# Down projection of a gated FFN: nine of eleven pairs of f tiles in a seven-product block form, with a transposed output turned back through DRAM

## The chip, the cores and the metric

The kernel runs on one core of a Trainium2 chip. The metric is the device time of one execution in microseconds (us). Three runs of the kernel before gave 745.83, 746.61 and 747.37 us; the median is 746.61.

## The reference

A layer on x of 2048 tokens and 512 channels: pre-norm attention with a compressive memory, then a pre-norm gated feed-forward, all in fp32. Cut to what matters:

```python
h  = x + attention(layernorm(x))          # 32 heads of 16, 4 segments of 512 tokens
g  = layernorm(h) @ w_gate                # 512 -> 1376
u  = layernorm(h) @ w_up                  # 512 -> 1376
h2 = h + (gelu(g) * u) @ w_down           # 1376 -> 512: the down projection
```

The change touches the last line.

## The kernel before, in words

**Precision.** Each fp32 matrix product is made of three matmuls in fp32r. An operand v is kept as a high part (a ScalarE copy to fp32r) and a low part (v minus the high part, a subtraction on GpSimd or VectorE); `SPLIT` lists high x high, high x low, low x high. So every operand of TensorE that is not a plain load costs a copy and a subtraction. The buffers for such pairs are the `slot`, `stk` and `stq` tiles, plain fp32 tiles of 128x512 are `row` and `vaug`, PSUM banks are `bank`.

**Stages.** The first part, some 390 us, is the attention. The second is the feed-forward (`ffn_weights`, `ffn`, `down`), in two halves p = 0, 1 of 1024 tokens; a half is two blocks s of 512 tokens. The 1376 inner channels are eleven f tiles: ten of 128, one (f = 10) of 96. The second layer norm of the second half (`layer_norm` and `ln2`, with a transposition through `t_dram`, L810 to L819) runs beside the first half of the feed-forward.

**Gate and up.** `ffn` computes gate and up of one f tile for both blocks s in a block form with seven products instead of eight (a Strassen-like scheme): weights a11, a12, a22, s1 to s4, made of gate and up by `ffn_weights` (splits at L1499 and L1501, sums of 256 columns at L1508), times activation blocks made by `ln2`. A product is two matmul groups of three: 7 x 2 x 3 = 42 matmuls per half and f tile, all at L1531. `geglu` (L1547 on) makes h = gelu(g) * u with ScalarE and VectorE, and splits it (ScalarE L1560, GpSimd L1563, for f = 9 VectorE).

**Down.** After a pair of f tiles (f = 10 alone, first pair (0,1), then 10, (2,3), up to (8,9)) `down` takes h as the stationary operand and w_down, split by `split_weight` (L666 to L675), as the moving one: for each of the eight blocks of 128 tokens of the half, three matmuls per f tile (L1596) into one PSUM bank, and one VectorE add into the block's row of sums (L1604), which began as h (L1626). With the last pair (8,9) the row is stored to `out` right after its add (L1609).

**What sets the order.** The program is recorded as operations with their dependencies and then issued in a fixed list, `ORDER`. Each engine works through its instructions strictly as that list gives them; buffers are handed out from pools in the same order. The DMAs are issued by SyncE (SP), but for one of the last stores, which ScalarE issues.

Of the kernel before, what the change touches and what calls it, by code (L numbers as in the profile page):

```python
# [7 lines left out]
F32 = mybir.dt.float32  # L8
# [3 lines left out]
OP = mybir.AluOpType  # L12
# [14 lines left out]
SPLIT = ((0, 0), (0, 1), (1, 0))  # L27

# [463 lines left out]
def infini_geglu(ctx: ExitStack, tc: tile.TileContext, x, wq, wk, wv, wo, beta,  # L492
# [1028 lines left out]
    def ffn(p, f, b):  # L1521
# [14 lines left out]
        def copy(src):  # L1536
            c = Val(PC)
            act(D, prio, lambda: nc.scalar.activation(c.t[:w], src.t[:w], AF.Copy), [src], [c])  # L1538
            return c
# [159 lines left out]
```

## Time and profile before

| what | before |
|---|---|
| median of three runs | 746.61 us |
| span of the profiled execution, first to last instruction | 745.2 us |
| runs above that span | 0.6 to 2.2 us, the median 1.4 |
| TensorE busy | 729.3 us, 98% |
| VectorE busy | 568.5 us, 76% |
| ScalarE busy | 511.5 us, 69% |
| GpSimd busy | 474.5 us, 64% |
| matmuls of gate and up (L1531) begin | 376.0 us |

The profiled execution is one run of its own, of which the span is known; the runs carry a little more around it. PE is TensorE, PEld its weight loads, DVE VectorE, ACT ScalarE, POOL GpSimd. An arrow `<-` stands between what is written and what is read; tile names come without their numbers in the profile.

### The profile page before, as it was taken

To read this page: it belongs to the slowest core of one execution; us is meant where nothing else is said; L and a number is where in the kernel's file an instruction comes from. 1 tells how busy PE (TensorE), PEld (TensorE's weight loads), DVE (VectorE), ACT (ScalarE), POOL (GpSimd) and SP (SyncE) were. 2 spreads that over 40 slices of the span, in tenths; PEclk is the share of its full clock that TensorE was granted. 3 is DMA by queue.
4 is the path that set the end of the run, shared out by engine and by line. 5 is a ranking of instruction groups with operands and counts; after the bars stand their busy time and mean duration, and the time that the engine had idled before them with its cause. 6 is when DMAs were issued, how large, how long until landed. Compare 5 with 4: busy or idle time off the path is not lost.

```text
span 745.2 us, 18708 instructions
## 1 busy us (share of the span) xinstructions
PE 729.3 (98%) x6496; PEld 582.5 (78%) x6496; DVE 568.5 (76%) x1812; ACT 511.5 (69%) x1078; POOL 474.5 (64%) x750
## 2 busy tenths in 40 slices
PE   7999999999999999999999999999999999999998
PEld 6887867777877777876768788888887878888886
DVE  6897879988887898899987547775688756565466
ACT  6898888797767878878676557755586453553641
POOL 5455425564536546876884887868797578659930
PEclk9999999999999999999999999999999999999999
DMA  7756647656657757776756685554334260000003
GB/s 268 203 142 163 173 127 190 177 131 189 175 155 206 211 155 200 185 219 197 194 186 219 215 258 158 108 134 103 106 106 129 67 210 19 0 1 1 0 1 113
DMA packets 89658, 107.92 MB, mean 145 GB/s; under 512 B 31468, under 2 KB 41884, under 8 KB 89564
## 3 DMA queue, kind: packets, MB, share of 16 engines
q1 hardware_dynamic: 89260, 106.34, 50.2%
q8 instruction: 51, 0.84, 0.5%
q10 hardware_dynamic: 304, 0.39, 0.2%
q14 instruction: 43, 0.35, 0.2%
HBM read 57.03 MB, written 23.53 MB: 108 GB/s over the span
## 4 chain that ended last, share of the span: by engine, by line
PE 86%; DVE 8%; ACT 2%; issue 2%; DMA 1%; SPq 0%; DVEq 0%; ACTq 0%
PE bank L1531 28%; PE bank L1596 15%; PE bank L932 9%; PE bank L1272 8%; PE bank L1244 6%; PE bank L1186 5%; PE bank L981 5%; PE bank L1352 3%; PE bank L1345 3%; DVE bank L1196 2%; DVE aside L1196 2%; PE bank L1154 1%; DMA row<-wq 1%; DVE nm L1196 1%; PE bank L798 1%
## 5 line engine op out<-in xcount | busy, mean ns | idle before, releaser
L1250 ACT ACTIVATE row<-bank 128x512 f32<-128x512 f32 x309 | 165.5, 604 | 29.8 <-PE bank L1244 25.4
L1258 POOL TENSOR_SCALAR_AFFINE_SELECT row<-row 128x256 f32<-128x256 f32 (+1 forms) x309 | 105.9, 367 | 89.9 <-ACT row L1250 87.6
L1196 DVE CUSTOM_DVE_ANT_0 aside<-bank,amask 128x384 f32<-128x384 f32 (+2 forms) x384 | 141.7, 419 | 17.4 <-PE bank L1186 10.2
L932 PE MATMUL bank<-slot,slot 64*128 64x512 f32 x720 | 114.3, 403 | 0.0
L1531 PE MATMUL bank<-slot,slot 128*128 128x512 f32 (+1 forms) x399 | 106.1, 391 | 0.0
L1196 DVE CUSTOM_DVE_ANT_0 bank<-bank,amask 128x512 f32<-128x512 f32 x128 | 86.5, 710 | 12.0 <-PE bank L1186 10.1
L1531 PEld LDWEIGHTS bank<-slot,slot 128*128 128x128 f32 (+1 forms) x399 | 73.6, 186 | 17.5 <-issue 0.4
L1501 POOL TENSOR_TENSOR slot<-row,slot 128x512 fp32r<-128x512 f32 (+2 forms) x55 | 61.6, 1125 | 39.9 <-ACT slot L1499 37.6
L1186 PE MATMUL bank<-stk,stq 64*128 64x512 f32 (+3 forms) x512 | 82.0, 331 | 2.6 <-DMA stq<-slot 0.9
L1244 PE MATMUL bank<-stq,stk 64*128 64x384 f32 (+3 forms) x512 | 81.4, 333 | 1.7 <-DVE nm L1196 0.8
L1604 DVE TENSOR_TENSOR row<-row,bank 128x512 f32<-128x512 f32 (+1 forms) x91 | 60.4, 677 | 29.6 <-PE bank L1596 29.2
L1272 PE MATMUL bank<-row,vaug 128*32 128x512 f32 (+3 forms) x988 | 78.8, 436 | 1.2 <-DVE z L1145 0.4
L932 PEld LDWEIGHTS bank<-slot,slot 64*128 64x128 f32 x720 | 73.0, 185 | 6.2 <-DVE nm L1196 0.7
L1186 PEld LDWEIGHTS bank<-stk,stq 64*128 64x128 f32 x512 | 56.5, 185 | 14.4 <-DVE nm L1196 3.7
L1244 PEld LDWEIGHTS bank<-stq,stk 64*128 64x128 f32 x512 | 56.1, 185 | 14.6 <-DVE nm L1196 3.7
L1596 PE MATMUL bank<-slot,slot 128*128 128x512 f32 (+1 forms) x228 | 59.8, 389 | 0.0
L1272 PEld LDWEIGHTS bank<-row,vaug 128*32 128x32 f32 x988 | 30.5, 109 | 34.3 <-issue 27.3
L1531 PE MATMUL bank<-stk,slot 128*128 128x512 f32 (+1 forms) x198 | 54.7, 389 | 0.0
L981 PE MATMUL bank<-slot,slot 64*128 64x256 f32 x672 | 53.4, 284 | 0.0
L672 POOL TENSOR_TENSOR slot<-row,slot 128x512 fp32r<-128x512 f32 (+1 forms) x33 | 42.6, 1293 | 16.0 <-ACT slot L667 15.8
L1538 ACT ACTIVATE row<-bank 128x512 f32<-128x512 f32 (+1 forms) x54 | 31.6, 594 | 28.3 <-PE bank L1531 27.3
L1196 DVE DVE_READ_ACCUMULATOR2_ANT nm<- 128x1 f32 x512 | 50.1, 98 | 0.0
(269 smaller groups left out, 1622.4 us busy)
## 6 DMA issues: line engine op xcount, KB each, us to landing
stq<-slot SPq DMA_DIRECT2D x96, 128.0 KB
stk<-slot SPq DMA_DIRECT2D x94, 128.0 KB
row<-x SPq DMA_DIRECT2D x31, 256.0 KB
pv_dram<-row SPq DMA_DIRECT2D x31, 256.0 KB
row<-r_dram SPq DMA_DIRECT2D x27, 256.0 KB
row<-h_dram SPq DMA_DIRECT2D x23, 256.0 KB
row<-wd SPq DMA_DIRECT2D x17, 256.0 KB
row<-wu SPq DMA_DIRECT2D x16, 256.0 KB
```

The lines of the kernel that those rows point to most:

```text
L932: return nc.tensor.matmul(pm[i].t, w[i].t[rows_of(r), wi, dc * P:(dc + 1) * P], XT[s][dc].t[rows_of(r), xi, :], start=(dc, wi, xi, ph) == ...
L981: return nc.tensor.matmul(pms[n].t[:, 256 * t:256 * t + 256], XT[s][dc].t[rows_of(r), xi, t0:t0 + P], whl[wi].t[rows_of(r), dc // 2, 256 * ...
L1186: nc.tensor.matmul(sa.t[:, c0:c0 + w], sq.t[own, p, i * P:(i + 1) * P], sk.t[own, p, 0:w], start=True, stop=True, tile_position=(64 * a, 0 ...
L1196: nc.vector.tensor_tensor_reduce(out=(sa.t[:, c0:c0 + w] if i > 2 else aside[:, turns[0]:turns[0] + w]), in0=sa.t[:, c0:c0 + w], in1=amask ...
L1244: nc.tensor.matmul(sc.t[:, c0:c0 + D - q0], sk.t[own, p, q0:q0 + P], sq.t[own, p, q0:D], start=True, stop=True, tile_position=(64 * a, 0), ...
L1250: act(w, prio, lambda sc=sc, e=e: nc.scalar.activation(e.t[:, :w], sc.t[:, :w], AF.Exp), [sc, vtab], [e])
L1258: nc.gpsimd.affine_select(v, v, pattern=pat + [[1, P]], compare_op=OP.is_ge, fill=0.0, base=0, channel_multiplier=-1)
L1272: nc.tensor.matmul(pv.t[32 * n:32 * n + 32, kb * P:D], va.t[:, 136 * kb + 17 * j:136 * kb + 17 * j + 32], e.t[:, lo:lo + D - kb * P], star ...
L1501: pool(0.14 + 2.13e-3 * (hi - lo), prio, lambda: nc.gpsimd.tensor_tensor(v.t[:, 1, :hi - lo], r.t[:, lo:hi], v.t[:, 0, :hi - lo].bitcast(F ...
L1531: nc.tensor.matmul(dst.t[:w], v.t[:, wi, c0 + j * w:c0 + (j + 1) * w], b[bk][j].t[:, xi, :], start=first and j == 0 and n == 0, stop=j == ...
L1596: nc.tensor.matmul(pm.t[:, cs], HH[p, f, s].t[:w, hi, t * P:(t + 1) * P], v.t[:w, wi, cs], start=f == fl[0] and n == 0, stop=f == fl[-1] a ...
L1604: dve(W_, prio, lambda a=a, pm=pm, cs=cs, to=to: nc.vector.tensor_tensor(to.t[:, cs], a.t[:, cs], pm.t[:, cs], op=OP.add), [pm, a], [to])
```

## The change

Nine pairs of f tiles take a new way: all five of the first half, and (0,1) to (6,7) of the second. The two single tiles f = 10 and the last pair (8,9) of the second half stay with `down`.

- **Seven products for down** (`down7`). The pair's two f tiles and the two token blocks s form a 2x2 block matrix b11, b12, b21, b22 of h; w_down of the pair is a 2x2 block matrix with 256 output channels to a block. w_down is now stationary and h the moving operand, so the output comes transposed: channels on partitions, tokens along the row. Seven products of 2 x 3 matmuls. VectorE makes four block differences (`sub`), each from two SBUF tiles; seven operands are split (ScalarE copy; low part on GpSimd, in the first three pairs of the first half two of the seven on VectorE). `geglu` no longer splits h for these tiles.
- **Gathering** (`gather`). Each product is added on VectorE from its PSUM bank into one of eight transposed sums; the first product of each sum is a ScalarE copy.
- **Weight blocks** (`wd_prep`, `wd_load`). In the first half GpSimd makes s1 to s4 of a pair (four operations of 256 columns), and all seven blocks are split (ScalarE and GpSimd, 256 columns each); of the first four pairs they go to `wd_dram`, from where the second half loads them. The input `wdp` is w_down with permuted columns, reordered on the host. Eight of the 35 `row` tiles become `half` tiles for the blocks (`halves`).
- **Turning back** (`turned`, `blocks_out`). Once the last pair of a half is gathered, VectorE turns 32x32 blocks (4 x 4 instructions of 128 columns per 512 tokens), 16 DMAs write them to `y_dram` so that the rest of the transposition falls into the addresses, and four loads bring them back by token. f = 10 has put its rows (h plus its share) into `g_dram`; these are loaded and added on GpSimd. In the first half the result is stored to `out`; in the second it is the row of sums to which the pair (8,9) is added before the store.
- The transposition of the second layer norm uses `blocks_out` too (16 short VectorE instructions where four long ones stood). The recorded cost of one VectorE step of the attention rises from 560 to 910, and `ORDER` is a new list for the whole program.

Three places in the order follow, each before and after; numbers behind names are buffers.

VectorE, first half, while the second layer norm of the other half runs. Before: the down adds (L1604) read a `row` tile and a bank, like the steps of `ffn` around them.

```order
L1543 TENSOR_TENSOR row_116<-row_116,bank_69 128x512
L1543 TENSOR_TENSOR bank_71<-row_129,bank_71 128x512
L1604 TENSOR_TENSOR row_135<-row_135,bank_72 128x512
L1604 TENSOR_TENSOR row_106<-row_106,bank_66 128x512
L1543 TENSOR_TENSOR bank_67<-vaug_145,bank_67 128x512
L1551 SCALAR_TENSOR_TENSOR row_129<-row_129,bank_71 128x512
L1604 TENSOR_TENSOR row_120<-row_120,bank_70 128x512
L1556 SCALAR_TENSOR_TENSOR bank_71<-row_129,bank_71 128x512
L1558 SCALAR_TENSOR_TENSOR row_129<-bank_71,row_116 128x512
L1604 TENSOR_TENSOR vaug_142<-vaug_142,bank_72 128x512
```

After, third pair: gathering adds are L1748, block differences L1711, low parts on VectorE L1718, short transposes L716.

```order
L1718 TENSOR_TENSOR slot_81<-row_109,slot_81 128x512
L812 SCALAR_TENSOR_TENSOR ln_167<-bank_70,ln_166 128x4
L1586 SCALAR_TENSOR_TENSOR row_104<-row_104,bank_72 128x512
L1588 SCALAR_TENSOR_TENSOR row_124<-row_124,bank_71 128x512
L1573 TENSOR_TENSOR bank_65<-vaug_140,bank_65 128x512
L1711 TENSOR_TENSOR row_109<-row_124,row_109 128x512
L716 STREAM_TRANSPOSE row_121<-row_134 128x4x32
L1581 SCALAR_TENSOR_TENSOR row_127<-row_127,bank_65 128x512
L1748 TENSOR_TENSOR row_111<-row_111,bank_70 128x512
L1748 TENSOR_TENSOR row_123<-row_123,bank_68 128x512
L748 TENSOR_SCALAR mv_160<-bn_158 128x1
```

The adds are gathering adds now, and between them stand operations that read two SBUF tiles (`row,row` and `row,slot`).

GpSimd, later in the first half. Before: weight splits (L1501), weight sums of 256 columns (L1508), splits of h (L1563).

```order
L1501 TENSOR_TENSOR slot_88<-row_115,slot_88 128x512
L1563 TENSOR_TENSOR stq_98<-vaug_143,stq_98 128x512
L1501 TENSOR_TENSOR slot_74<-row_104,slot_74 128x512
L1508 TENSOR_TENSOR vaug_141<-row_107,vaug_141 128x256
L1508 TENSOR_TENSOR vaug_141<-vaug_141 128x256
L1501 TENSOR_TENSOR slot_86<-row_130,slot_86 128x256
L1501 TENSOR_TENSOR slot_85<-row_107,slot_85 128x512
L1508 TENSOR_TENSOR row_130<-row_130 128x256
L1563 TENSOR_TENSOR stq_97<-row_114,stq_97 128x512
L1508 TENSOR_TENSOR row_130<-row_132,row_130 128x256
L1501 TENSOR_TENSOR slot_84<-row_132,slot_84 128x512
```

After: splits of the blocks of h (L1718), gate and up as before (L1526), and w_down's block sums (L1679) and block splits (L1687).

```order
L1718 TENSOR_TENSOR slot_80<-row_111,slot_80 128x512
L1679 TENSOR_TENSOR row_127<-row_127,row_134 128x256
L1718 TENSOR_TENSOR stq_96<-row_109,stq_96 128x512
L1526 TENSOR_TENSOR slot_85<-row_120,slot_85 128x512
L1526 TENSOR_TENSOR stq_99<-row_115,stq_99 128x512
L1718 TENSOR_TENSOR slot_73<-row_124,slot_73 128x512
L1687 TENSOR_TENSOR half_6807<-row_121,half_6807 128x256
L1718 TENSOR_TENSOR slot_84<-row_105,slot_84 128x512
L1526 TENSOR_TENSOR slot_80<-row_108,slot_80 128x512
L1687 TENSOR_TENSOR half_6812<-row_101,half_6812 128x256
L1718 TENSOR_TENSOR stq_96<-row_125,stq_96 128x512
```

The operations that prepare w_down have come in between, and there are more splits of h.

SyncE at the end of the program. Before: one weight load and the stores of the rows.

```order
L1494 DMA row_102<-wg 128x512
L1609 DMA out_dram<-row_113 128x512
L1609 DMA out_dram<-row_111 128x512
L1609 DMA out_dram<-row_109 128x512
L1609 DMA out_dram<-row_120 128x512
L1609 DMA out_dram<-row_121 128x512
L1609 DMA out_dram<-row_125 128x512
L1609 DMA out_dram<-row_130 128x512
```

After: writes of the turned blocks (L720), their loads (L1774), a store of the first half (L1778); the stores of the last rows follow.

```order
L720 DMA y_dram<-row_124 32x4x128
L720 DMA y_dram<-row_112 32x4x128
L720 DMA y_dram<-row_124 32x4x128
L1774 DMA row_127<-y_dram 128x512
L720 DMA y_dram<-row_112 32x4x128
L720 DMA y_dram<-row_104 32x4x128
L720 DMA y_dram<-row_112 32x4x128
L1774 DMA row_113<-y_dram 128x512
L1778 DMA out_dram<-row_119 128x512
L1774 DMA row_111<-y_dram 128x512
L1774 DMA row_123<-y_dram 128x512
L1774 DMA row_109<-y_dram 128x512
```

The stores of the last rows, which stood behind the last adds alone, now stand behind writes to `y_dram` and the loads that wait for them.

The core of the diff:

```diff
-    P2 = Pool_(many("row", 35, [P, D]))
+    P2 = Pool_(row_t)
+    half_t = [[] for _ in range(NHALF)]
+    PWD = Pool_(half_t)
...
+    def blocks_out(prio, tiles, to, v):
+        for k in range(4):
+            q = Val(PN)
+            for c, x in enumerate(tiles):
+                dve(130, prio, lambda q=q, c=c, x=x, k=k: nc.vector.transpose(
+                    q.t.rearrange("p (b c j) -> p b c j", b=4, c=4)[:, :, c],
+                    x.t[:, k * P:(k + 1) * P].rearrange("p (b i) -> p b i", b=4)), [x], [q], chain=True)
+            for a in range(4):
+                dma(prio, lambda q=q, k=k, a=a: nc.sync.dma_start(bass.AP(
+                    tensor=to.tensor, offset=to.offset + k * P * D + a * P, ap=[[D, 32], [32 * D, 4], [1, P]]),
+                    q.t[32 * a:32 * a + 32].rearrange("p (b x) -> p b x", b=4)), [q], [v], kb=70, dur=0.5, chain=True)
...
+    def wd_prep(n):
...
+        for d, a, c, ins, o in (((sa, 0), (ra, 1), (rb, 1), raw, OP.add), ((sa, 1), (sa, 0), (ra, 0), [ra], OP.subtract),
+                                ((sb_, 0), (ra, 0), (ra, 1), [ra], OP.subtract),
+                                ((sb_, 1), (rb, 0), (sa, 1), [rb, sa], OP.subtract)):
...
+            act(256, prio, lambda v=v, c0=c0, w=w: nc.scalar.activation(w.t[0][:, 0], half(v, c0), AF.Copy), [v, vhalf], [w],
+                src=0.092)
+            pool(0.14 + 2.13e-3 * 256, prio, lambda v=v, c0=c0, w=w: nc.gpsimd.tensor_tensor(
+                w.t[0][:, 1], half(v, c0), w.t[0][:, 0].bitcast(F32), op=OP.subtract), [v], [w])
+            if n < BY7[1]:
+                dma(prio, lambda w=w, k=k: nc.sync.dma_start(
+                    wd_dram[n, k], w.t[0].bitcast(F32)), [w], [WDD[n][k]])
...
+    def down7(p, n):
+        b11, b12, b21, b22 = [HH[p, 2 * n + i, s] for i in range(2) for s in range(2)]
...
+        def sub(d, a, c):
+            dve(D, prio, lambda: nc.vector.tensor_tensor(d.t, a.t, c.t, op=OP.subtract),
+                [v for v in (a, c) if v is not d], [d])
...
+        sub(t1, b12, b11)
+        h = {"11": split(b11), "t1": split(t1)}
+        sub(t2, b22, t1)
+        h["t2"] = split(t2, dve if p == 0 and n < 3 else pool)
+        h["21"] = split(b21)
+        sub(b12, b22, b12)
+        h["t3"] = split(b12)
+        h["22"] = split(b22)
+        sub(t2, b21, t2)
+        h["t4"] = split(t2, dve if p == 0 and n < 3 else pool)
...
+                    for m, (wi, xi) in enumerate(SPLIT):
+                        nc.tensor.matmul(dst[u].t, ws[a].t[0][:, wi, P * u:P * u + P], h[bk].t[:, xi], start=first and m == 0,
+                                         stop=m == 2, skip_group_check=True)
...
+                    dve(D, prio, lambda u=u, acc=acc: nc.vector.tensor_tensor(acc.t, acc.t, src[u].t, op=OP.add),
+                        [src[u]], [acc])
...
+        prod("a11", "11", X, True)
+        gather(X, 0, 0)
+        prod("a12", "21", Z, True)
+        gather(Z, 0, 0)
...
+    def turned(p):
+        for s in range(2):
+            blocks_out(prio, [ACCT[p][dc // 2, dc % 2, s] for dc in range(ND)], y_dram[2 * p + s], v)
+            for t in range(4):
...
+                dma(prio, lambda r=r, n=n: nc.sync.dma_start(r.t, g_dram[n * P:n * P + P]), [GD[n]], [r])
+                dma(prio, lambda y=y, s=s, t=t: nc.sync.dma_start(y.t, y_dram[2 * p + s, t * P:t * P + P]), [v], [y])
+                pool(1.24, prio, lambda r=r, y=y: nc.gpsimd.tensor_tensor(r.t, r.t, y.t, op=OP.add), [y], [r])
+                LAST[n] = r
...
```

More of the change, by code (lines that the diff above doesn't have):

```diff
@@ new lines, in tokens, with halves, f @@
+    def tokens(x, p, s, t, cs=slice(0, D)):
+        r0 = (8 * p + 4 * s) * P
+        if p == 0:
+            return x[r0 + t * P:r0 + t * P + P, cs]
+        return bass.AP(tensor=x.tensor, offset=x.offset + (r0 + 32 * t) * D + cs.start,
+                       ap=[[P * D, 4], [D, 32], [1, cs.stop - cs.start]])
+    vhalf = Val()
+    def halves():
+        held = [Val(P2) for _ in half_t]
+        def f():
+            for v, h in zip(held, half_t):
+                i = next((i for i, t in enumerate(row_t) if t is v.t))
+                h.append(p0.tile([P, 2, 256], F32R, name=f"half{i}", tag=f"row{i}"))
+            nc.gpsimd.memset(tick, 0.0)
+        pool(0.1, at(0, 0), f, [], [vhalf], acq=held)
+        for v in held:
+            v.users += 1
@@ L1652, in infini_geglu @@
             ffn(p, f, B[p])
[L1653 to L1655 removed]
+            if by7(p, f) and f % 2 == 0:
+                WDV[p, f // 2] = wd_load(p, f // 2)
+            elif by7(p, f):
+                down7(p, f // 2)
+                if f == 2 * BY7[p] - 1:
+                    turned(p)
+            elif f == 10:
+                down(p, (10,), acc(p))
+            elif f % 2:
+                down(p, (f - 1, f), [LAST[8 * p + i] for i in range(8)])
     return S.run(ORDER)
```

130 lines of the change are left out of this document (102 added, 28 removed), and 529 rows, old and new, of the table ORDER.

## The prediction

> **What bounds the kernel now.** I read the page's engine shares first, then the windows of the feed-forward stage, TensorE's waits and the chain of waits.
>
> ```profile
> PE 729.3 (98%) x6496; PEld 582.5 (78%) x6496; DVE 568.5 (76%) x1812; ACT 511.5 (69%) x1078; POOL 474.5 (64%) x750
> 425.00:450.00 25.00, 25.00 (x112) 20.62 (x111) 13.98 (x34) 14.56 (x33) 19.30 (x20) 1.00 0.78 255
> 525.00:550.00 25.00, 25.00 (x112) 20.68 (x112) 16.48 (x27) 18.38 (x37) 23.24 (x24) 1.00 0.36 106
> 550.00:575.00 25.00, 24.36 (x107) 19.50 (x106) 23.77 (x37) 17.11 (x33) 19.50 (x20) 1.00 0.40 124
> 650.00:675.00 25.00, 25.00 (x112) 20.68 (x111) 15.06 (x24) 15.18 (x29) 13.74 (x12) 1.00 0.00 1
> PE bank L1531 <- DVE row L1604: 0.6, 1, 0.6
> 641.58 21.77 PE bank L1531 x96
> 677.62 8.16 PE bank L1596 x36
> ```
>
> Columns of the windows: busy time of TensorE, its weight loads, VectorE, ScalarE, GpSimd, then the granted clock. From about 392 us on TensorE is busy in every microsecond, at full clock, and the single row of its waits (0.6 us) is all that it waited for there. So the stage is bound by the number of matmuls. The chain gives their price: 21.77 / 96 = 0.2268 us for gate and up (L1531), 8.16 / 36 = 0.2267 us for down (L1596). But the other engines are not far off: GpSimd has windows of 23.24 of 25 us, VectorE one of 23.77.
>
> **What the change removes.** A pair of f tiles took 2 x 8 x 3 = 48 down matmuls, the block form takes 7 x 2 x 3 = 42, of the same shape (128x128 weights, 512 columns). Nine pairs: 54 matmuls fewer x 0.2267 = **12.2 us**, all on the path as long as TensorE stays the bound. Everything else below is what may eat it.
>
> **What it adds beside TensorE.** Durations from these rows; for queues I take start to start.
>
> ```profile
> L1604 DVE TENSOR_TENSOR row<-row,bank 128x512 f32<-128x512 f32 x89 | 59.6, 683 | 28.4 <-PE bank L1596 28.1
> 561.06 1.27 DVE L1604 TENSOR_TENSOR row<-row,bank 128x512 f32<-128x512 f32 x2
> 562.25 0.68 DVE L1558 SCALAR_TENSOR_TENSOR row<-row,bank 128x512 f32<-128x512 f32 x1
> L1145 DVE STREAM_TRANSPOSE z<-bank x12: 216/218/218, 81.2 to 352.7; 128x32 f32<-128x32 f32 x12
> 675.89 1.30 POOL L1563 TENSOR_TENSOR slot<-row,slot 128x512 fp32r<-128x512 f32 x1
> 677.13 0.76 POOL L1501 TENSOR_TENSOR slot<-vaug,slot 128x256 fp32r<-128x256 f32 x1
> 677.83 1.32 POOL L1501 TENSOR_TENSOR stq<-vaug,stq 128x512 fp32r<-128x512 f32 x1
> ```
>
> VectorE: two adds in 562.25 - 561.06 = 1.19 us, 0.60 each. It gets 110 gathering adds, 36 subtractions and 6 splits, and loses 72 old adds and 2 splits: 78 x 0.60 = 47 us, and 96 short transposes for 8 long ones, some 17 us at 0.24 each (the row of 0.22 us for 32 columns and 0.60 for 512 enclose it). 64 us more over 315 us of matmuls: from some 16 to 21 of 25 us on average, so hidden but for the crowded places. ScalarE gets some 28 us more on 15 of 25 us; hidden.
>
> GpSimd: a subtraction of 512 columns takes 1.25 us (675.89 to 677.13), one of 256 takes 0.70 (677.13 to 677.83). The first half of the tokens prepares the new weight blocks (55 operations of 256 columns) and splits seven operands a pair instead of four. I counted what the new order lists on GpSimd from 9.9 us of products to the operand that is used at 188.0 us (products at 0.2267): 77 of 512 columns, 109 of 256, four smaller ones. That is 77 x 1.25 + 109 x 0.70 + 1.9 = 174.4 us of work for 178.1 us of products. The old order has 77 and 50 there, about 133 us. So GpSimd has almost no room left in the first half.
>
> **The stall that the change brings.** The 36 subtractions and 6 splits on VectorE read both operands from SBUF. The kernel before has four such operations in the stage. One ran while GpSimd was busy:
>
> ```profile
> 568.37 1.84 DVE L1563 TENSOR_TENSOR slot<-row,slot 128x512 fp32r<-128x512 f32 x1
> 568.37 1.28 POOL L1563 TENSOR_TENSOR slot<-row,slot 128x512 fp32r<-128x512 f32 x1
> 569.62 1.72 POOL L1397 TENSOR_TENSOR slot<-row,slot 128x512 fp32r<-128x512 f32 x1
> 573.26 0.69 DVE L1563 TENSOR_TENSOR slot<-row,slot 128x512 fp32r<-128x512 f32 x1
> 574.76 1.30 POOL L1397 TENSOR_TENSOR stq<-vaug,stq 128x512 fp32r<-128x512 f32 x1 [3.43 <-ACT stq L1392]
> ```
>
> Both started at 568.37. VectorE took 1.84 us instead of 0.69, to 570.21, half a microsecond past the end of GpSimd's operation, and GpSimd's next then took 1.72 instead of 1.30: 0.42 us lost there. At 573.26 GpSimd was idle (3.43 us up to 574.76) and the same operation took 0.69. So each of them costs VectorE up to 1.15 us (0.57 in the mean, for a random moment of GpSimd's operation) and GpSimd 0.42 us, when GpSimd is never idle. The L1604 adds read one operand from PSUM and show 0.68 throughout; the new gathering adds are of that kind.
>
> 26 of the 42 stand in the stretch counted above. GpSimd then needs 174.4 + 26 x 0.42 = 185.3 us, and about 0.5 us to hand on, against 178.1: 7.7 us late, and TensorE waits for it. VectorE's loss in the same stretch (26 x 0.57 = 15 us on 141 of 178) runs beside it. In the second half the weight blocks come ready from DRAM, and GpSimd has room; for late bank releases there I take 1.0 us (0 to 2). Bounds for the whole stall: nothing if GpSimd finds room that I don't see, which leaves 1 us; above, 0.60 instead of 0.42 at each (VectorE's whole operation), 174.4 + 15.6 + 0.5 - 178.1 = 12.4 us.
>
> The Trainium skill, "SBUF — State Buffer", section "Who interferes with whom", says that such an instruction "contends with a GpSimd instruction that reads SBUF", and that the pair of ports is an exclusive lock for the whole instruction, so that whoever comes second is blocked until the first ends. By that rule, GpSimd's price would be up to VectorE's 0.60 us, where the row shows 0.42: 12.4 us of delay by the rule, 7.7 by the row. I go by the row.
>
> **The end.** Of the second half, eight rows of sums now wait for y_dram: last gathering add, transposes, 16 writes per 512 tokens, loads, GpSimd adds, the old adds, the stores.
>
> ```profile
> 735.24 7.30 SPq L1609 DMA_DIRECT2D out_dram<-row  x8
> 741.13 0.52 PE L1596 MATMUL bank<-stq,stq 128*128 128x256 f32 x3
> 491.46 1.58 SPq L814 DMA_DIRECT2D t_dram<-vaug  x3
> 533.62 0.43 SPq L814 DMA_DIRECT2D t_dram<-vaug  x1
> 536.48 0.33 SPq L819 DMA_DIRECT2D row<-t_dram  x1
> SPq L819 <- DMA t_dram<-vaug: 2.3, 1, 2.3
> ```
>
> Before, TensorE ends at 741.65, the last store is issued by 742.54 and the span ends at 745.2: 3.55 us behind TensorE, 2.66 of them the landing. After, the last write of y_dram leads to: 2.9 us until its readers may load (533.62 to 536.48, of which SyncE waited 2.3), 0.4 and 2.7 for a load (landing as that of the store), four GpSimd adds 5.0, an add 0.7, a store 3.1: 14.8 us. The last transposes stand 70 matmuls, 15.9 us, ahead of the end; of the last 16 DMAs ahead of that write, 8 need them, at 0.53 each (1.58 / 3) 4.2 us. So the last write falls 11.7 us before TensorE's end, 9.7 if VectorE is 2 us late: the span ends 3.1 to 5.1 us behind TensorE. I take **+1.0** (0 to 1.6). If SyncE runs only as its rows stand among the matmuls, the last write falls at TensorE's end: +11.3.
>
> **Attention** keeps its instructions in another order. Its waits are short:
>
> ```profile
> PE bank L869 <- DMA row<-x: 3.9, 1, 3.9
> PE bank L1186 <- DMA stq<-slot: 0.9, 1, 0.9
> PE bank L1272 <- DVE z L1145: 0.4, 1, 0.4
> ```
>
> Beyond the first load nothing there is over 0.9 us, so there is little to win and, with the same engines as full as before, a like amount to lose: 0, from -2 to +2. SyncE's 158 further DMAs, at 0.53 us, are 84 us on a queue with gaps, and 28 weight loads stand at least 14 matmuls (3.2 us) ahead of their use: nothing, up to 1 us if one lands late.
>
> **Sum.** -12.2 + 7.7 + 1.0 + 1.0 + 0 = **-2.5** us, against the profiled execution: span 745.2 to 742.7. The median of the runs, 746.61, lies 1.4 above that span, and I keep that: **744.1 us**. From no change a measurement can tell about 0.2%, 1.5 us.
>
> **Rivals.**
> - *The stall is absorbed* (0.22). For it: VectorE has 37 us to spare in the stretch, and TensorE's operands are mostly listed long before their use. Against it: GpSimd is listed at 174 of 178 us. Left are 1 us of GpSimd's own, 0.5 at the end: -12.2 + 1.5 + 1 = -9.7, 736.9 us.
> - *Slower: GpSimd pays the full operation* (0.20). Place: the first half, up to the weights and operands of its last pair. Price: 0.60 at each of 26, 12.4 us of waiting. It turns the saving into a loss once GpSimd loses over 0.52 us each time (26 x 0.52 - 3.2 = 10.2, which with the 2.0 from above is the saving). At 0.60: -12.2 + 12.4 + 2 = +2.2, and +5 if VectorE's late bank releases add some 3: 748.8 to 751.6. For it: one sample only carries 0.42. This is the Trainium skill's rule ("SBUF — State Buffer", same section) in its full form; the single row here shows less.
> - *Slower: the turned output ends last* (0.09): -12.2 + 7.7 + 1 + 11.3 = +7.8, 754.4. For it: the rows' places among the matmuls. Against it: SyncE's 0.53 us.
> - *The saving is not there* (0.05): were matmuls of the block form dearer than 0.2267, or the attention order 4 us worse: +1 to +3, 747.6 to 749.6. Against it: L1531 and L1596 cost the same.
>
> **How the numbers follow.** My forecast has 0.44; its own range is 740.5 to 748 (delay from 4 to 11 us). Over 1.5 us faster are some 0.26 of these and the 0.22 of the first rival: 0.48. Within: 0.12 and some 0.05 of the others, 0.17. Slower: 0.06, 0.20, 0.09, in all 0.35. Low end 736.0, where the stall is absorbed; high end 751.5, the full price, which leaves out the turned output and a part of each edge.
>
> **What would show it.** In the profile after: 0.2267 us a matmul in the chain and 54 fewer; new two-SBUF operations on VectorE with a mean well over 0.69 us (I expect 1.1 to 1.3), GpSimd's 512-column operations above 1.30 in the mean; GpSimd at 24 to 25 of 25 us in the windows of the first half, and TensorE waiting there for GpSimd and for banks, 6 to 10 us in all, little in the second half; TensorE to span end 3.5 to 5 us. Wrong if TensorE waits for nothing there (first rival), or if the end is over 8 us behind it.

## The result, and the profile after

| | before | after |
|---|---|---|
| median of four runs | 746.22 us (745.45 to 747.37) | 785.74 us (783.71 to 789.37) |
| span of the profiled execution | 745.2 | 782.0 |
| TensorE's last matmul ends | 741.65 | 753.24 |
| from there to the end of the span | 3.55 | 28.7 |

The ratio is 1.0534 (95% interval 1.0504 to 1.0563): slower by 5.3%, where 744.1 us and at most 751.5 were forecast.

The first thing to read is the end of the program. SyncE's timeline of the kernel after, its last rows, then two rows of VectorE's and one of TensorE's (start, duration, both in us):

```profile
741.88 0.43 SPq L1774 DMA_DIRECT2D row<-y_dram  x1
752.03 0.36 SPq L1778 DMA_DIRECT2D out_dram<-row  x1
752.43 1.87 SPq L1774 DMA_DIRECT2D row<-y_dram  x4
754.35 1.21 SPq L1641 DMA_DIRECT2D out_dram<-row  x2
755.66 0.96 SPq L1778 DMA_DIRECT2D out_dram<-row  x1
757.47 10.73 SPq L1641 DMA_DIRECT2D out_dram<-row  x6
756.76 3.14 DVE L1636 TENSOR_TENSOR row<-row,bank 128x512 f32<-128x512 f32 x5 [6.86 <-POOL row L1775]
760.43 0.69 DVE L1636 TENSOR_TENSOR row<-row,bank 128x512 f32<-128x512 f32 x1 [0.54 <-POOL row L1775]
749.66 3.58 PE L1628 MATMUL bank<-stq,slot 128*128 128x512 f32 x15
```

Two things are late here. SyncE issues nothing from 742.3 to 752.03, and its last four loads of y_dram stand behind that hole, so VectorE's last add ends at 761.1 and not with TensorE. And from 761.1 there is nothing left but stores, yet the span ends at 782.0: 21 us, where a landing took 2.66 before. The windows of that time (the columns are as in the prediction; the last two are the DMA engines' share and GB/s) and SyncE's waits from 740 us on (us in total, times, the longest):

```profile
765.00:770.00 5.00, 0.00 (x0) 0.00 (x0) 0.00 (x0) 0.00 (x0) 0.00 (x0) 0.50 0.26 100
770.00:775.00 5.00, 0.00 (x0) 0.00 (x0) 0.00 (x0) 0.00 (x0) 0.00 (x0) 0.50 0.26 102
```

```profile
SPq L1876 <- DMA out_dram<-row: 12.7, 1, 12.7
SPq L1778 <- DMA out_dram<-row: 9.7, 1, 9.7
```

The stores move at 102 GB/s with a DMA share of 0.26: 4 of 16 engines' worth. Eight rows of 256 KB at that rate are 20.6 us.

The second thing is TensorE. Its matmuls cost what they did, 2.04 / 9 = 0.2267 us in both products (rows of the chain of waits), and the page counts 54 fewer (x6442 for x6496):

```profile
PE 726.2 (93%) x6442; PEld 569.7 (73%) x6442; DVE 648.4 (83%) x1978; ACT 534.3 (68%) x1138; POOL 554.0 (71%) x827
```

```profile
722.85 2.04 PE bank L1561 x9
724.89 2.04 PE bank L1737 x9
```

So the 12.2 us are saved. But TensorE ends 11.6 us later than before, and so has lost 11.6 + 12.2 = 23.8 us. Where, the windows of the feed-forward tell (length, then busy time and matmuls of TensorE), first of the kernel after, then of the kernel before:

```profile
412.00:625.00 213.00, 206.40 (x888) 163.04 (x888) 179.85 (x348) 148.04 (x301) 205.12 (x207) 1.00 0.56 173
625.00:753.25 128.25, 122.44 (x532) 97.97 (x531) 107.87 (x182) 61.41 (x112) 102.87 (x89) 1.00 0.63 194
```

```profile
412.00:625.00 213.00, 212.36 (x933) 172.44 (x932) 144.73 (x254) 130.55 (x256) 164.11 (x162) 1.00 0.49 138
625.00:741.65 116.65, 116.65 (x520) 96.53 (x518) 72.39 (x113) 54.21 (x98) 70.40 (x66) 1.00 0.04 13
```

The busy time is too kind here, since a matmul that starts after a wait looks longer; the counts are better. In 412 to 625 TensorE does 888 matmuls for 933: 45 x 0.2267 = 10.2 us lost. From 625 on it took 116.65 / 520 = 0.2243 us a matmul before; 532 of those are 119.3 us, and it took 128.25: 8.9 lost. The other 23.8 - 19.1 = 4.7 us are lost up to 412 us, in the attention and its last crossing with the feed-forward. With the end, 28.7 - 3.55 = 25.2 us later behind TensorE, the parts are -12.2 + 4.7 + 10.2 + 8.9 + 25.2 = 36.8 us, the difference of the spans (4.7 is what is left over, so the sum has to close).

Theories for it: **1**, transfers in 4 groups of 32 rows run on 4 DMA engines (the stores of the second half, and the loads of h_dram that begin its sums); **2**, SyncE's wait for the half row that ScalarE stores; **3**, the two-SBUF stall; **4**, the attention's new order. Their rivals stand in the expectations.

### The profile page after: what moved, and what is told of

The parts are those of the page before. It is cut to its first block, busy times and chain, and to the rows that moved or that the text cites. A ratio compares the mean times of both kernels' runs of the same rounds, so it can differ in the third digit from the quotient of the medians.

```text
span 782.0 us, 19221 instructions
## 1 busy us (share of the span) xinstructions
PE 726.2 (93%) x6442; PEld 569.7 (73%) x6442; DVE 648.4 (83%) x1978; ACT 534.3 (68%) x1138; POOL 554.0 (71%) x827
## 4 chain that ended last, share of the span: by engine, by line
PE 22%; DVE 13%; POOL 10%; DMA 5%; issue 4%; ACT 2%; SPq 1%; POOLq 0%; DVEq 0%; ACTq 0%
PE bank L1561 12%; PE bank L1737 4%; DVE row L1748 2%; DVE row L1711 2%; POOL slot L1718 2%; POOL row L1533 2%; DMA g_dram<-row 2%; PE bank L1377 2%; PE bank L1297 1%; POOL half L1687 1%; POOL stq L1526 1%; POOL row L1775 1%; DVE bank L1573 1%; DVE row L1581 1%; POOL slot L1526 1%
## 5 line engine op out<-in xcount | busy, mean ns | idle before, releaser
L1221 DVE CUSTOM_DVE_ANT_0 aside<-bank,amask 128x256 f32<-128x256 f32 (+2 forms) x384 | 141.0, 419 | 15.4 <-PE bank L1211 11.0
L1561 PE MATMUL bank<-slot,slot 128*128 128x512 f32 (+1 forms) x354 | 95.2, 392 | 0.7 <-ACT vaug L1568 0.7
L1269 PE MATMUL bank<-stq,stk 64*128 64x128 f32 (+3 forms) x512 | 81.7, 337 | 1.6 <-DVE bank L767 0.4
L1748 DVE TENSOR_TENSOR row<-row,bank 128x512 f32<-128x512 f32 x110 | 71.5, 675 | 10.8 <-PE bank L1737 9.4
L1297 PE MATMUL bank<-row,vaug 128*32 128x256 f32 (+3 forms) x1024 | 78.1, 436 | 1.1 <-DVE nm L1221 0.6
L957 PEld LDWEIGHTS bank<-slot,slot 64*128 64x128 f32 x720 | 70.8, 185 | 5.9 <-DVE tock L562 0.4
L1526 POOL TENSOR_TENSOR slot<-row,slot 128x512 fp32r<-128x512 f32 (+3 forms) x56 | 65.6, 1176 | 6.3 <-ACT slot L1524 5.7
L1269 PEld LDWEIGHTS bank<-stq,stk 64*128 64x128 f32 x512 | 55.3, 185 | 13.3 <-DVE nm L1221 3.5
L1737 PE MATMUL bank<-slot,half 128*128 128x512 f32 x216 | 58.2, 393 | 3.5 <-DVE row L1748 3.3
L1561 PE MATMUL bank<-slot,stq 128*128 128x512 f32 (+1 forms) x180 | 50.5, 393 | 1.8 <-POOL stq L1526 1.2
L1737 PEld LDWEIGHTS bank<-slot,half 128*128 128x128 f32 x216 | 40.0, 188 | 14.0 <-DVE row L1748 5.6
L1006 PEld LDWEIGHTS bank<-slot,slot 64*128 64x128 f32 x672 | 47.5, 186 | 1.4 <-DVE z L1170 0.4
```

The source lines that it names most:

```text
L957: return nc.tensor.matmul(pm[i].t, w[i].t[rows_of(r), wi, dc * P:(dc + 1) * P], XT[s][dc].t[rows_of(r), xi, :], start=(dc, wi, xi, ph) == ...
L1006: return nc.tensor.matmul(pms[n].t[:, 256 * t:256 * t + 256], XT[s][dc].t[rows_of(r), xi, t0:t0 + P], whl[wi].t[rows_of(r), dc // 2, 256 * ...
L1221: nc.vector.tensor_tensor_reduce(out=(sa.t[:, c0:c0 + w] if i > 2 else aside[:, turns[0]:turns[0] + w]), in0=sa.t[:, c0:c0 + w], in1=amask ...
L1269: nc.tensor.matmul(sc.t[:, c0:c0 + D - q0], sk.t[own, p, q0:q0 + P], sq.t[own, p, q0:D], start=True, stop=True, tile_position=(64 * a, 0), ...
L1297: nc.tensor.matmul(pv.t[32 * n:32 * n + 32, kb * P:D], va.t[:, 136 * kb + 17 * j:136 * kb + 17 * j + 32], e.t[:, lo:lo + D - kb * P], star ...
L1526: pool(0.14 + 2.13e-3 * (hi - lo), prio, lambda: nc.gpsimd.tensor_tensor(v.t[:, 1, :hi - lo], r.t[:, lo:hi], v.t[:, 0, :hi - lo].bitcast(F ...
```

## The experiments

Each time is the median of four or more runs, beside runs of the kernel before on the same chip (746.3 to 747.8). The changed kernel is at 785.7; a repeat of it gave 784.3 (below), so a difference under 2 us says little.

**Stores in 4 groups (theory 1).** In `tokens`, the second half's store goes to 4 groups of 32 rows (`[P * D, 4], [D, 32]`).

```diff
-  dst = ... else tokens(out, p, s, t, cs)
+  dst = ... else out[n * P:n * P + P, cs]
```

> Only the address pattern of the second half's stores to out is changed: 128 rows one behind the other instead of 4 groups of 32 rows (the rows of the output are permuted by that; bytes, order, queues and waits are the same). Theory 1 (a store whose outermost dimension is 4 is moved by 4 of the 16 DMA engines, some 100 GB/s, and eight of them need 20 us): the last add still ends some 8 us behind TensorE, and the stores land 3 us later, so the end lies 11 to 13 us behind TensorE instead of 28.8, and the time falls by 15 to 18 us to 768 to 771. Rival (the stores are late only because the adds are, or because eight come at once): less than 4 us, 782 or more.

Measured: 767.4 us, 18.3 less. The last add ended at 761.3, as in the changed kernel, but the stores behind it kept pace:

```profile
755.00:760.00 5.00, 0.00 (x0) 0.00 (x0) 3.13 (x5) 0.00 (x0) 4.41 (x4) 0.96 0.99 351
```

All 16 engines, 351 GB/s (the last loads of y_dram are among it), and the end 10.4 us behind TensorE (754.9 to 765.3). The same pattern by itself, put into the kernel before the change, which has no late adds:

```diff
-  out[r0:r0 + P, cs], to.t[:, cs]
+  rows_at(r0, cs), to.t[:, cs]      # second half: ap=[[P * D, 4], [D, 32], [1, ...]]
```

> The kernel before the change with one edit: the second half's stores to out go to 4 groups of 32 rows, as in the changed kernel (the output's rows are permuted); nothing else. Theory 1 by itself: TensorE ends where it did (741.7), 2.1 MB at some 102 GB/s from 735.5 us on last until 756, and the time rises by 11 to 13 us, to 758 to 761. Rival (the slow stores of the changed kernel come from its late adds or its full queue): within 2 us of before.

Measured: 762.4 us against 747.0, ratio 1.0208 (1.0182 to 1.0233). TensorE ended at 745.0 in this profile, the span at 764.6, with the share and rate of the changed kernel between:

```profile
750.00:755.00 5.00, 0.00 (x0) 0.00 (x0) 0.00 (x0) 0.00 (x0) 0.00 (x0) 0.50 0.27 102
755.00:760.00 5.00, 0.00 (x0) 0.00 (x0) 0.00 (x0) 0.00 (x0) 0.00 (x0) 0.50 0.26 102
```

Late adds or a full queue are not needed for it. Two more shapes tell the number of groups from the jumps between them:

```diff
-  ap=[[P * D, 4], [D, 32], [1, ...]]
+  ap=[[64 * D, 8], [D, 16], [1, ...]]       # and [[32 * D, 16], [D, 8], [1, ...]]
```

> The kernel before the change, the second half's stores to out in 8 groups of 16 rows (output rows permuted). If the number of groups, the outermost dimension, sets how many engines work on a store: 8 of 16, a DMA share of 0.5 and some 200 GB/s behind TensorE's end, 2.1 MB in 10.5 us from 738.5 on; the end lies 5 to 8 us behind TensorE (19.5 with 4 groups, 3.6 with plain rows) and the time is 749 to 752. If the jumps between the groups are what costs (8 groups have twice as many), it is no faster than with 4 groups, 762.

> The same with 16 groups of 8 rows. By the number of groups: all 16 engines, the end 3 to 5 us behind TensorE, the time within 2 us of the kernel before. By the jumps: 762 or more.

Measured: 752.2 us with 8 groups (ratio 1.0077, 1.0052 to 1.0102), 747.0 with 16 (1.0004, 0.9988 to 1.0020). With 8 groups, right behind TensorE's end:

```profile
741.00:745.00 4.00, 0.00 (x0) 0.00 (x0) 0.39 (x1) 0.00 (x0) 0.00 (x0) 1.00 0.52 192
```

The DMA share is 0.26 with 4 groups, 0.52 with 8 and full with plain rows; the rates are 102, 192 and 380 GB/s (the last with stores of plain rows alone in flight, from 755 to 758 us of the run with both edits further down). The number of groups sets it, and more jumps cost nothing that shows in the time. The Trainium skill, "DMA: Bandwidth & Descriptors", section "Why a DMA increments its semaphore by 16 and not by 1", says just this: the number of engines is the largest k up to 16 that divides the sizes of the slowest dimension on both sides. The three shares here agree with it.

**The half row (theory 2).** A first attempt moved ScalarE's store of the half row in the list.

> Only one store moves in the list: the half row that ScalarE stores comes behind SyncE's last load of y_dram. Theory 2 (SyncE waited 9.7 us for that store to land, because the store that SyncE issues takes the same one of eight places for DMAs in flight): the wait is gone, the last y loads issue at about 743 instead of 752.4, and the last add ends with TensorE, about 755. If theory 1 holds too, the stores still need 20 us from about 750 on, so the end lies 18 to 22 us behind TensorE and the time falls by only 7 to 11 us, to 775 to 779. If the wait alone made the end late, it lies 4 to 6 us behind TensorE and the time falls by 23, to 763.

> Both edits together: plain rows for the second half's stores, and the half row's store behind the y loads (rows of the output permuted). Theories 1 and 2 together: the end lies 3 to 6 us behind TensorE, as the prediction had it, and the time falls by 23 to 26 us, to 760 to 763. Rival (something else ends late, for instance the turned output itself, whose last write SyncE issues at 741.8): still over 8 us behind TensorE.

Measured: 784.3 and 765.9 us. Neither is a test: the store stood behind the y loads in the list already, and the edit left every engine's instructions and waits as they were. They count as repeats of the changed kernel (785.7) and of plain rows (767.4). What the wait comes from shows in the program's own list for SyncE: each DMA takes one of eight semaphores in turn, and waits until the one before it with the same semaphore has landed.

```
764 L720 DMA y_dram_183<-row23_124 32x4x128 [waits DMAHW5_49]
765 L720 DMA y_dram_183<-row11_112 32x4x128 [waits DMAHW7_49]
772 L1778 DMA out_0_dram<-row18_119 128x512 [waits DMAHW6_49]
773 L1774 DMA row10_111<-y_dram_183 128x512 [waits DMAHW7_49]
```

Number 6 between 764 and 765 went to ScalarE's half row, which cannot be stored before TensorE is nearly done. So 772, a store of the first half that had time, waits for it, and the y loads wait behind 772. ScalarE's timeline has the half row's store just before SyncE's hole ends at 752.03:

```profile
748.64 1.14 ACTq L1641 DMA_DIRECT2D out_dram<-row  x1
```

The edit that reaches it:

```diff
-  q = nc.scalar if i else nc.sync
+  q = nc.sync
```

> The half row that ScalarE stored is stored by SyncE, at its place in the list behind the y loads; nothing else changes (the output is right). Theory 2: SyncE no longer waits some 10 us for that store ahead of its last four y loads; they issue at about 743 to 745 and the last add ends with TensorE, near 754. With theory 1 (the stores of 4 groups of 32 rows run at some 102 GB/s; 2.1 MB are 20.5 us, from about 749.5 on) the end still lies 16 to 19 us behind TensorE, and the time falls by 9 to 13 us against the changed kernel, to 773 to 777. If the wait were only a shadow of those slow stores, the time stays within 3 us.

> Plain rows for the second half's stores and the half row stored by SyncE (rows of the output permuted). Theories 1 and 2 together: the last add ends with TensorE, the stores land 3 us later, the end lies 4 to 6 us behind TensorE instead of 28.7, and the time falls to 760 to 763, some 6 below plain rows alone (767.4). Rival (something else of the turned output is late, its loads or GpSimd's adds): 8 us or more behind TensorE, 765 or more.

Measured: 779.8 us (6 less than the changed kernel, where 9 to 13 were expected) and 761.3 (6 less than plain rows, as expected). In both the hole is gone. SyncE's timeline with both edits:

```profile
743.98 0.45 SPq L1778 DMA_DIRECT2D out_dram<-row  x1
744.47 2.25 SPq L1774 DMA_DIRECT2D row<-y_dram  x4
750.32 1.78 SPq L1641 DMA_DIRECT2D out_dram<-row  x3
752.69 3.44 SPq L1641 DMA_DIRECT2D out_dram<-row  x6
```

The loads issue at 744.5 instead of 752.4, and the span ends 4.7 us behind TensorE (754.9 to 759.6). That is the prediction's "3.1 to 5.1": the turned output itself is in time. With the slow stores kept (first edit alone) the six last stores began to issue at 754.3, not at the 749.5 of the expectation, and ran at 102 GB/s to the end, 23.0 us behind TensorE; that start is where the estimate was off.

**The two-SBUF operations (theory 3).**

```diff
-  nc.vector.tensor_tensor(d.t, a.t, c.t, op=OP.subtract)
+  nc.vector.transpose(d.t, a.t)        # and the six splits on VectorE likewise
```

> The 36 subtractions and 6 splits on VectorE with two SBUF operands are replaced by transpositions of 32x32 blocks of one SBUF operand at the same place, about as long when alone (0.6 us); the values are wrong by that. Theory 3 (the two-SBUF operations and GpSimd hold each other up and make most of the 18.7 us by which TensorE waits more in the feed-forward): the new operations take 0.60 to 0.70 us, GpSimd's operations stay at 1.30, TensorE's idle time between 412 us and its end falls from 21 to 8 to 12 us, and the time falls by 9 to 13 us, to 773 to 777. Rival (these waits come from the length of VectorE's and GpSimd's lists or from late DMAs, not from the stall): less than 3 us, 783 or more.

Measured: 772.5 us, 13.3 less. Groups of 412 to 760 us, in the changed kernel and then here (busy time, mean ns):

```profile
L1711 DVE TENSOR_TENSOR row<-row,row 128x512 f32<-128x512 f32 x36 | 41.1, 1153 | 1.6 <-DMA h_dram<-row 0.8 <-DMA g_dram<-row 0.4
L1748 DVE TENSOR_TENSOR row<-row,bank 128x512 f32<-128x512 f32 x110 | 71.5, 675 | 10.8 <-PE bank L1737 9.4 <-issue 1.1
L1718 POOL TENSOR_TENSOR slot<-row,slot 128x512 fp32r<-128x512 f32 x31 | 42.3, 1367 | 1.4 <-ACT slot L1716 1.4
L1718 POOL TENSOR_TENSOR stq<-row,stq 128x512 fp32r<-128x512 f32 x16 | 23.4, 1463 | 0.4 <-ACT stq L1716 0.4
```

```profile
L1711 DVE STREAM_TRANSPOSE row<-row 128x512 f32<-128x512 f32 x36 | 24.8, 698 | 1.8 <-POOL stq L1718 0.8 <-DMA g_dram<-row 0.6
L1718 POOL TENSOR_TENSOR slot<-row,slot 128x512 fp32r<-128x512 f32 x31 | 40.1, 1298 | 1.9 <-ACT slot L1716 1.6 <-DMA half<-wd_dram 0.2
L1718 POOL TENSOR_TENSOR stq<-row,stq 128x512 fp32r<-128x512 f32 x16 | 20.6, 1293 | 0.9 <-ACT stq L1716 0.8
```

The adds with a PSUM operand (L1748) take 0.675 throughout; the subtractions (L1711) take 1.153 in the mean, as predicted (1.1 to 1.3), and GpSimd's operations go up to 1.46. With one SBUF operand all of it is gone, and TensorE ends at 743.4 instead of 753.2.

**The loads in 4 groups (theory 1 again).**

```diff
-  a[i].t, tokens(h_dram, p, s, t)
+  a[i].t, h_dram[(n + t) * P:(n + t + 1) * P]
```

> Only the eight loads of h_dram that begin the second half's sums read plain rows instead of 4 groups of 32 rows (the output's rows get the wrong h). Theory 1 for loads: they too run on 4 engines, hold places among the eight DMAs in flight at 617 to 640 us, and so hold up the loads and stores behind them; TensorE's idle time from 625 us on (9.2 us, of it 3.7 between 625 and 650) falls by 3 to 5 us, and the time by as much, to 781 to 783. Rival (the waits there come from VectorE and GpSimd alone): no change within 1.5 us.

Measured: 780.0 us, 5.8 less (3 to 5 were expected). In the changed kernel SyncE's writes of y_dram waited for these loads (SyncE's waits from 600 to 650 us), and TensorE was idle for 3.7 us of a window:

```profile
SPq L720 <- DMA row<-h_dram: 4.0, 2, 2.4
```

```profile
625.00:650.00 25.00, 21.33 (x90) 16.30 (x90) 19.06 (x32) 11.55 (x22) 15.78 (x15) 1.00 0.64 197
```

With plain rows:

```profile
625.00:650.00 25.00, 25.00 (x111) 20.61 (x110) 21.05 (x34) 13.78 (x27) 19.39 (x18) 1.00 0.79 251
```

SyncE no longer waits for these loads in that stretch, and 21 more matmuls stand in the same 25 us.

**All of it at once.**

> All that was found so far is taken out at once: plain rows for stores and loads, SyncE's store of the half row, one SBUF operand instead of two in VectorE's 42 operations (rows permuted and values wrong). If the causes add up: TensorE ends 10 us earlier without the two-SBUF stall and 2 to 4 earlier with plain loads, at 739 to 742, the end 4.7 behind it, and the time is 745 to 749, that is the saving of 12.2 us less some 5 in the attention, some 5 to 6 of waits of other kinds and 1 at the end. Rival (a further cause that only shows together): over 752.

Measured: 742.1 us against 747.0, ratio 0.995 (0.993 to 0.997). That is 0.5% faster than the kernel before, for a version that leaves out the block differences and so does not compute the reference, and 3 us better than the estimate. The windows of its feed-forward:

```profile
412.00:625.00 213.00, 211.71 (x927) 171.44 (x926) 176.95 (x364) 151.61 (x310) 199.06 (x211) 1.00 0.59 183
625.00:735.31 110.31, 110.21 (x491) 90.93 (x489) 94.14 (x172) 56.28 (x103) 97.31 (x89) 1.00 0.73 224
```

927 matmuls for 933 before, and 110.31 / 491 = 0.2247 us each from 625 on: TensorE is the bound again. So the waits of the feed-forward are the stall and the grouped transfers, and nothing else of size. GpSimd at 199 of 213 us is no bound as long as nobody stops it.

**The right output without the transfers.** Three versions compute the reference without them. In the first two a store or load in 4 groups is four DMAs of 32 rows:

```diff
-  q.dma_start(tokens(out, p, s, t, cs), to.t[:, cs])
+  for b in range(4):
+      r0 = (8 + 4 * s + b) * P + 32 * t
+      (nc.sync, nc.scalar)[b % 2].dma_start(out[r0:r0 + 32, cs], to.t[32 * b:32 * b + 32, cs])
```

> The changed kernel with the right output and without the two transfers of theory 1: each store of the second half is four DMAs of 32 rows (two from SyncE, two from ScalarE, so that the half row no longer has a place of its own ahead of the y loads), each of the eight h loads four DMAs of 32 rows from SyncE. Theory 1 and 2: the end lies 5 to 9 us behind TensorE (some 36 issues of 0.4 us on two queues), TensorE's idle time from 625 us on falls from 9 to 6, and the time falls by 20 to 27 us, to 759 to 766: still slower than before, by the waits of the feed-forward and the attention. Rival (splitting costs as much in issues and places as it wins): over 770.

> The changed kernel with the right output: full rows of the second half stored as four DMAs of 32 rows on two queues, both half rows by SyncE as 4 x 32 rows of 256 columns, h loads in four DMAs of 32 rows. Against the first mended version (768.6, where the y loads still waited until 749.6 for ScalarE's parts of the half row) the y loads issue at 743 to 745; the end lies 7 to 10 us behind TensorE (15.0 there) and the time is 760 to 764. If the eight places for DMAs in flight bound the end even so (28 small DMAs and the loads), it stays at 767 to 769.

Measured: 768.6 and 765.2 us; both miss their ranges (759 to 766 and 760 to 764). In the first the y loads again waited (to 749.6) for a piece of the half row on ScalarE; in the second, with the half rows on SyncE, they issued at 740.8, and the end was still 10.0 us behind TensorE. Many small DMAs are no good substitute: SyncE alone took 7.45 us to issue the last twelve. Whether the eight places or the issues themselves bound them was not separated. The third takes away what makes the groups: the tokens of the second half are only out of order because the new transposition writes runs of 512 B.

```diff
-  vector.transpose of 4 x 4 parts; writes ap=[[D, 32], [32 * D, 4], [1, P]]
+  vector.transpose(q.t, x.t), once per row tile; writes ap=[[D, 32], [32 * D, 16], [1, 32]]   # second layer norm only
-  tokens: 4 groups of 32 rows for p == 1
+  tokens: plain rows for both p; the half row stored by SyncE
```

> The changed kernel with the right output and no transfer in 4 groups: the second layer norm's transposition goes back to 8 long VectorE instructions and writes of 128 B runs as before the change, so that the second half's tokens stand in their own order and its h loads and stores are plain rows; the half row is stored by SyncE. If theories 1 and 2 add up (plain stores and the half row 24.4 us below the changed kernel, plain loads 5.8): the end 4 to 6 us behind TensorE and the time 755 to 758. What is then left against the kernel before is the two-SBUF stall (13 us by its own experiment) and the attention, less the saving. If the longer writes' return or a wait that only shows now eats it: 760 or more.

Measured: 755.6 us, ratio 1.0131 (1.0101 to 1.0160): 30 us below the changed kernel, as the causes add up, and still 9 above the kernel before. No version with the right output beat it; one would have to do without the two-SBUF subtractions, and that was not tried.

**The attention (theory 4).** Its 3009 operations are the same in both kernels, so a list of the kernel before can be put into the changed one.

> The 3009 operations of the attention stand in the order of the kernel before (9 of them moved, by up to 3 places); the other operations keep the changed kernel's order among them and their places between (the output is right). Theory 4 (the 5 us that TensorE loses up to 412 us come from the new order of the attention): TensorE's time outside the feed-forward's matmuls up to 412 us falls from 392 to 394 (all profiles of the changed kernel so far) to 388 to 390, and the time by 3 to 5 us, to 781 to 783. Rival (the loss comes from what was added beside the attention, weights and block preparation on GpSimd and the queue): 392 to 394 as before, and the time within 2 us.

> The first 2100 of the attention's 3009 operations stand in the order of the kernel before (to about 250 us), the other ones nearly in the changed kernel's. Theory 4, as the last run bore it out up to 275 us (matmul 3600 began at 273.3 there, 274.4 before the change, 276.8 in the changed kernel): TensorE is 2 to 3 us earlier at 250 us than in the changed kernel and keeps that, and the time falls by 2 to 3 us, to 782 to 784. Rival (what is won in the attention is lost where feed-forward work stands between): within 1 us, or slower.

> The first 1000 operations of the attention in the order of the kernel before, all operations behind the 1500th of the list at their places in the changed kernel's order (the output is right). If the new order's first part costs TensorE (matmul 1200 began at 103 to 105 us in that order, at 105 to 106.7 in the changed kernel's): matmul 1200 at 103 to 104.5, kept to the end, the time 1 to 3 us below the changed kernel, 782.5 to 784.5. If a later stretch makes up for it anyhow: within 1 us.

Measured: 824.1, 844.5 and 789.6 us. TensorE's window up to 250 us, in the kernel before, the changed one, and the first of these:

```profile
0.00:250.00 250.00, 241.22 (x3221) 191.35 (x3223) 210.71 (x901) 203.89 (x463) 128.12 (x305) 1.00 0.64 178
```

```profile
0.00:250.00 250.00, 239.47 (x3198) 191.91 (x3198) 213.58 (x910) 200.41 (x456) 123.52 (x298) 1.00 0.61 165
```

```profile
0.00:250.00 250.00, 242.61 (x3233) 192.95 (x3235) 212.13 (x907) 204.88 (x464) 128.41 (x307) 1.00 0.63 175
```

With the old order TensorE is 3.1 us busier up to 250 us than with the new one. The other profiles with the new order lie between 239.0 and 241.3 us in this window, so 1 to 3 us there are the order's. But the two lists do not fit each other further on, and far more is lost from 250 to 275 us on (in the last version from where the two lists meet, at 104 to 137 us). The three expectations of a gain failed. Of the 4.7 us up to 412 us, a part is thus the new order; how much of the rest is the preparation of the weight blocks at the crossing stays open.

## Why the prediction was wrong

- **The saving, -12.2.** Right: 54 matmuls fewer at 0.2267 us.
- **The end, +1.0.** This failed first and by most: 25.2 us. The step that failed is the price of the stores, "a store 3.1", together with a wait that the sum does not have. The price was taken from rows of plain stores, while the diff shows another address pattern for the same bytes; in 4 groups the stores cost 18.3 us more. And the loads of y_dram were taken to issue as soon as their writes had landed, while they stood behind ScalarE's half row, which cost 6.1. The chain of the turned output, its writes, loads and adds, was sized right: 4.7 us with both removed. The prediction's own sign, "if the end is over 8 us behind it", was met.
- **The rival "the turned output ends last"** gave 754.4 for late writes. The writes were in time (the last at 741.84); the loads behind them were not, held by a wait across two queues that the timing among matmuls does not show.
- **The stall, +7.7 and +1.0.** The mechanism was right, and so was the price on GpSimd. Over all its instructions from 412 us on (300 in both), GpSimd is busy 312.92 us in the changed kernel and 297.10 with one SBUF operand. That is 15.8 us, or 0.38 for each of the 42 operations, where 0.42 was predicted. The sums of the windows from 412 us to the end, the changed kernel first:

```profile
sum 378.00, PE 328.84 PEld 261.01 DVE 291.54 ACT 209.45 POOL 312.92; mean PE 109.61 PEld 87.00 DVE 97.18 ACT 69.82 POOL 104.31
sum 378.00, PE 325.76 PEld 263.30 DVE 272.98 ACT 209.38 POOL 297.10; mean PE 108.59 PEld 87.77 DVE 90.99 ACT 69.79 POOL 99.03
```

The delay of the first half came out as forecast: from 425 to 625 us TensorE does 832 matmuls in the changed kernel and 867 with one SBUF operand, and 35 x 0.2267 = 7.9 us, for 7.7. The term of the second half was too small: 8.9 us are lost there against 118.43 - 504 x 0.2243 = 5.4 with one SBUF operand, so 3.5 us, for 1.0 (0 to 2). (TensorE's end itself came only 9.8 us earlier: that run was some 1.6 us later already at 425 us, where the edit has changed nothing yet.) The step that did not hold is that VectorE's loss in that stretch "runs beside it". VectorE lost (1.153 - 0.698) x 36 = 16 us on the subtractions, 0.46 each (0.57 predicted), and a part of it is on TensorE's path. Of the waits that the trace names for TensorE in the feed-forward, the longest in total are:

```profile
PE bank L1737 <- DVE row L1748: 3.3, 3, 1.9
PE bank L1628 <- DVE row L1636: 2.2, 2, 1.2
PE bank L1561 <- POOL stq L1526: 1.2, 1, 1.2
PE bank L1737 <- DVE row L1586: 1.2, 2, 0.9
```

The second row belongs to the loads in 4 groups: it is gone with plain loads (theory 1) and stays with one SBUF operand. The first row is VectorE's gathering adds, which release the banks. But the engine that came last need not be the one that was late: the chain of waits runs almost wholly through GpSimd from 430 to 476 us, and through VectorE's operations on two SBUF operands right behind that.

```profile
473.31 1.25 POOL slot L1526
474.55 1.24 POOL stq L1526
477.82 1.70 DVE slot L1718
479.55 2.81 DVE row L1711 x2
```

So both engines hold TensorE up. How much each costs is not shown, since the experiment frees both at once; and since the 7.7 counted GpSimd's delay alone, that 7.9 comes so near to it is in part luck. The Trainium skill's rule ("SBUF — State Buffer", section "Who interferes with whom") holds in that both engines are held up and that the stall goes when the second SBUF operand goes; read as VectorE's whole 0.60 us on GpSimd, it would have been further off than the row's 0.42.

- **VectorE's further work.** The 96 short transposes took 0.283 us each, not 0.24, and 96 x 0.24 less 8 x 0.60 is 18.2 us, not 17; nothing in the sum hangs on it.
- **SyncE's queue, "nothing, up to 1 us if one lands late".** The loads in 4 groups held the queue at 617 to 640 us: 3.5 us of TensorE's end, 5.8 of the median. Again a pattern, not a count of issues.
- **Attention, 0 from -2 to +2.** 4.7 us, outside its own bounds.
- **Taken together**: without the two grouped transfers and the half row's place (and with the second layer norm's old transposition) the kernel stands at 755.6, 4 us above the range's 751.5. Left in it are the attention and a stall somewhat larger than forecast. The range failed on what was not priced at all.

## What to carry to other kernels

When a change gives a transfer another address pattern, price it as a new transfer, even where bytes and partitions are the same: look first at the outermost dimension on both sides. A store that one engine issues late can stop another engine's queue far ahead of it, where both take from the same few places for DMAs in flight. And a stall between two engines holds up both: follow each of them to the engine that is the bottleneck, also the less busy one.

## What the runs showed of the hardware

- The rate of a store by its outermost dimension: 4 groups 102 GB/s (DMA share 0.26), 8 groups 192 GB/s (0.52), plain rows 380 GB/s (1.02, with stores alone in flight).
- Where a VectorE subtraction with two SBUF operands meets GpSimd it takes 1.153 us in the mean; the same 512 columns as a transposition with one operand take 0.698, and the add from PSUM 0.675. GpSimd's operations rise from 1.29 to 1.46 us in the worst group, and over all of them GpSimd loses 15.8 us, 0.38 for each of VectorE's 42 operations.
- SyncE's store with the semaphore that ScalarE's store had taken before it waited 9.7 us for that store; with both stores on SyncE's queue the wait was gone.
